# Spectral filter and 32-head attention on one core: GpSimd freed of its recurring work, and filler matmuls moved to another PSUM bank

## The chip, the cores and the metric

The kernel runs on one core of one Trainium2 chip. The metric is device time in microseconds from the first to the last instruction of the core; the figure for the kernel before is the median of three executions, and a profile of one further execution is used for the reading.

## The reference

Two independent computations of one input length, S = 2048 rows of D = 640, are joined along the last axis.

```python
def _A_ref(x, w_r, w_i):                      # part A: spectral filter
    X = rfft2(x.astype(float32), axes=(-2, -1))
    X = X * (w_r + 1j * w_i)
    return irfft2(X, s=(S, D), axes=(-2, -1)).astype(bfloat16)

def _B_ref(x, wqkv, wo):                      # part B: attention, H = 32, Dh = 20
    q, k, v = split of (x @ wqkv) by 3, heads, Dh
    p = softmax(q k^T * Dh ** -0.5)
    return (p v, heads joined) @ wo

return concatenate([A, B], axis=-1)           # 1 x 2048 x 1280, bf16
```

## The kernel before, in words

Part B is the bulk. A unit is a pair of a chunk of 512 queries and a group of 4 heads: 4 chunks by 8 groups give 32 units, each of 64 score tiles (16 key tiles by 4 heads) of 128 keys by 512 queries. A score tile is a row-tiled matmul (32 of the array's 128 rows, one head, L1724). It is turned into an exponential in one of two ways. ScalarE takes groups of 3 and 2 tiles at once from banks 0 to 2 and 3 to 5 of PSUM (L1741). VectorE takes tiles in pairs from bank 7 or 5: an eviction for each (L1814) and seven steps for the pair (L1851 to L1864) that build the exponential's bits. The exponentials meet the values in column-tiled matmuls of 32 columns a head (L1906), four heads side by side, which add up in bank 6 for the whole unit. Column 20 of each head's values is a one, so the sum of the exponentials comes out in the same bank.

A unit ends with a chain. `unit_copy` copies bank 6 to SBUF (L1925). Four small DMAs spread the sums over partitions. `unit_recip` takes their reciprocals and two extremes on VectorE (L1943 to L1946). One DMA writes them to DRAM and another spreads them over 32 partitions a head. `unit_norm` multiplies (L1964, on GpSimd in the kernel before) into `OTn`, which the output projection reads (L1986).

Part A is the 2-D transform as matmuls in stages S1 to S11. S2 loads the filter weights `Wn`, GpSimd re-lays them into `Wl` (L1104), and TensorE transposes them into `Wp` (L1121). S1 and S3 to S5 transform the input along both axes, with `Bl` transposed into `BT` by the same helper `flip_jobs`. S6 and S7 finish the forward transform and multiply by the filter (L1262, L1267, L1274). S8 to S11 go back, with `U` transposed into `UT` by `flip_jobs`. All of them are background jobs, as are the projections of Q, K and V.

The order on each engine is fixed when the program is built. The class `FK` plays the kernel on a planner's clock: `occupy` books an engine for a planned duration, `at` sets due times, and `dispatch` picks what an engine does next. For TensorE the choice is, in order, scores, a lone VectorE tile, more of a running background job (`more_bg`, up to `RUN` pieces), values, the tail, a new background job, and last `warm`, a filler matmul. `warm` and the start of background jobs of part A look at `share`, the planned use of the array over the last stretch, and act where it is at or below `WARM_SHARE`. Each engine then executes its list strictly in that order and waits on semaphores. So an instruction that waits holds up everything behind it on its engine, whatever the planner thought.

The change and the prediction also speak of `setup_B` (loads, memsets L1496 to L1515, and the padding of Q and K weights from 20 to 32 columns a head, L1511 on ScalarE for group 0 and L1513 on GpSimd for the rest), `mk_jobs_B_static` (the K projection, L1546), `job_QA` (L1623), `dummy2` (the filler, L1610) and `copy_on` (every eviction by VectorE, L227).

A second program, the class `KB`, follows for inputs whose sums leave a checked range; a flag at the end skips it here, and it takes no part in the profile.

## Time and profile before

| What | Value |
|---|---|
| time, three runs | 1002.08 us median, 969.36 to 1003.15 |
| span of the profiled run | 1016.1 us, mean granted clock of TensorE 0.844 |
| PE busy | 886.0 us (87%), 5981 matmuls |
| VectorE (DVE) busy | 838.2 us (82%), 1633 instructions |
| ScalarE (ACT) busy | 848.8 us (84%), 743 instructions |
| GpSimd (POOL) busy | 73.2 us (7%), 56 instructions |
| score tiles | 1806 on ScalarE in 723 groups, 242 on VectorE in 121 pairs |
| idle time of ScalarE before L1741 | 139.9 us, of it 81.7 for scores and 56.5 for values |
| wait of the reciprocal L1943 for its DMA | 25.9 us, 27 times |
| filler matmuls L1610 | 99 weight loads |

Busy shares are means over stretches that differ much, so they don't tell what limits a stretch; the slices and the stretches do. A group's row gives the line, the engine, the operation, shapes and count, then busy time and mean duration, then the idle time of the engine just before it and what ended that. In a timeline the bracket after an instruction is the idle time before it and what released it. PEclk is the granted clock of TensorE[...].

### The profile page before, as it was taken

The page shows a single profiled execution, that of the slowest core. Times are in us where ns is not written, and L with a number is a line of the kernel's source. Part 1 is how long each engine was busy: PE and PEld are TensorE (multiplying, and loading weights), DVE is VectorE, ACT ScalarE, POOL GpSimd, SP SyncE. Part 2 cuts the span into 40 slices and gives each one's busy share as a digit, 9 for nine tenths or more (in the row PEclk, how much of TensorE's full clock was granted, in tenths as well). Part 3 has the DMA queues.
Part 4 walks back from the last instruction along what each step waited for, and adds up shares of the span by engine and source line. Part 5 has one row for each costly group of instructions (what it writes and reads, how often), then busy time and mean ns, then how long its engine had stood idle before and what let it go on. Part 6 is the DMA issues. An engine that isn't in the chain of part 4 may idle for free.

```text
span 1016.1 us, 14983 instructions
## 1 busy us (share of the span) xinstructions
PE 886.0 (87%) x5981; PEld 279.4 (27%) x6045; DVE 838.2 (82%) x1633; ACT 848.8 (84%) x743; POOL 73.2 (7%) x56
## 2 busy tenths in 40 slices
PE   8898989779998898887999888788989999997897
PEld 4332322113233232222332111232222332222112
DVE  5677999997779898999977888888887997679983
ACT  6599988777989998999985887699887998679882
POOL 5100010220000000000000000000010010000000
PEclk9699999886779999999995877799776997579757
DMA  6240000002200000110000000101010011100000
GB/s 202 60 92 12 12 2 11 12 15 84 65 19 31 12 13 12 43 43 12 12 24 15 12 12 0 53 12 53 12 40 18 31 38 38 37 26 12 12 12 28
DMA packets 31824, 31.75 MB, mean 31 GB/s; under 512 B 13444, under 2 KB 26500, under 8 KB 31492
## 3 DMA queue, kind: packets, MB, share of 16 engines
q1 hardware_dynamic: 31748, 30.73, 10.3%
q8 instruction: 48, 0.79, 0.3%
q14 instruction: 28, 0.23, 0.1%
HBM read 24.97 MB, written 5.50 MB: 30 GB/s over the span
## 4 chain that ended last, share of the span: by engine, by line
PE 37%; DVE 36%; ACT 15%; DMA 4%; SPq 4%; issue 3%; ACTq 0%; DVEq 0%
ACT arena L1741 14%; PE ps L1724 12%; PE ps L1906 8%; DVE arena L227 6%; DVE arena L1814 6%; DMA arena<-arena 4%; SPq L361 4%; DVE arena L1855 4%; DVE arena L1859 3%; PE ps L1340 3%; DVE arena L1862 3%; DVE arena L1864 3%; DVE arena L1851 2%; DVE arena L1857 2%; DVE arena L1853 2%
## 5 line engine op out<-in xcount | busy, mean ns | idle before, releaser
L1741 ACT ACTIVATE arena<-ps 128x1536 bf16<-128x1536 f32 x723 | 837.6, 1257 | 139.9 <-PE ps L1724 81.7
L1724 PE MATMUL ps<-arena 32*128 32x512 bf16 x2048 | 344.0, 434 | 66.3 <-ACT arena L1741 41.6
L1906 PE MATMUL ps<-arena 128*32 128x512 bf16 (+1 forms) x2048 | 231.1, 444 | 15.4 <-DVE arena L1864 13.1
L1814 DVE TENSOR_SCALAR arena<-ps 128x512 uint16<-128x512 f32 x242 | 165.5, 684 | 56.5 <-PE ps L1724 55.7
L227 DVE CAST arena<-ps 128x320 bf16<-128x320 f32 (+4 forms) x262 | 146.3, 559 | 39.1 <-PE ps L1340 11.6
L1724 PEld LDWEIGHTS ps<-arena 32*128 32x128 bf16 x2048 | 74.9, 93 | 282.3 <-ACT arena L1741 175.7
L1964 POOL TENSOR_TENSOR arena<-arena 128x512 bf16<-128x512 f32 x31 | 46.4, 1496 | 881.2 <-DMA arena<-rscr 789.4
L1906 PEld LDWEIGHTS ps<-arena 128*32 128x32 bf16 (+1 forms) x2048 | 52.5, 94 | 168.1 <-issue 123.4
L1855 DVE TENSOR_TENSOR arena<-arena 128x1024 f16<-128x1024 f16 x121 | 87.7, 725 | 1.7
L1862 DVE TENSOR_TENSOR arena<-arena 128x1024 uint16<-128x1024 uint16 x121 | 87.5, 723 | 0.7
L1859 DVE TENSOR_TENSOR arena<-arena 128x1024 f16<-128x1024 f16 x121 | 84.1, 695 | 1.6
L1864 DVE TENSOR_SCALAR arena<-arena 128x1024 uint16<-128x1024 uint16 x121 | 60.2, 498 | 0.4
L1851 DVE TENSOR_SCALAR arena<-arena 128x1024 uint16<-128x1024 uint16 x121 | 55.3, 457 | 0.5
L1853 DVE TENSOR_SCALAR arena<-arena 128x1024 f16<-128x1024 int16 x121 | 53.3, 441 | 1.2
L1857 DVE TENSOR_SCALAR arena<-arena 128x1024 f16<-128x1024 f16 x121 | 53.0, 438 | 1.1
L1340 PE MATMUL ps<-arena 128*128 128x320 bf16 (+1 forms) x192 | 52.4, 389 | 0.7 <-DVE arena L227 0.3
L1623 PE MATMUL ps<-arena 128*128 128x512 bf16 x135 | 47.4, 434 | 2.1 <-issue 1.3
L1546 PE MATMUL ps<-arena 128*128 128x512 bf16 x144 | 45.2, 410 | 2.8 <-DVE arena L227 0.8
L227 DVE COPY arena<-ps 128x1024 bf16<-128x1024 bf16 (+2 forms) x54 | 33.3, 620 | 17.3 <-PE ps L539 8.0
L1986 PE MATMUL ps<-arena 128*128 128x320 bf16 x192 | 40.2, 322 | 1.6 <-DVE arena L1814 1.5
L1610 PE MATMUL ps<-arena 128*128 128x512 bf16 x85 | 36.2, 462 | 5.2 <-DVE arena L1814 4.3
L1179 PE MATMUL ps<-arena 128*128 128x328 bf16 x160 | 35.4, 320 | 5.1 <-DVE arena L1814 3.9
(74 smaller groups left out, 469.6 us busy)
## 6 DMA issues: line engine op xcount, KB each, us to landing
arena<-rscr SPq DMA_DIRECT2D x31, 256.0 KB
arena<-in_B_x_dram SPq DMA_DIRECT2D x4, 640.0 KB, 6.5
arena<-in_A_x_dram SPq DMA_DIRECT2D x4, 640.0 KB, 4.5
out_dram<-arena SPq DMA_DIRECT2D x16, 160.0 KB, 1.8
out_dram<-arena SPq DMA_DIRECT2D x4, 640.0 KB, 3.6
arena<-in_B_wqkv_dram SPq DMA_DIRECT2D x3, 700.0 KB, 9.6
arena<-f_ciCS SPq DMA_DIRECT2D x2, 1024.0 KB, 5.3
arena<-arena SPq DMA_DIRECT2D x124, 2.0 KB, 1.7
```

Of the source, the lines that this page charges most:

```text
L227: return eng.tensor_copy(out, in_)
L1340: return lambda e: e.matmul(o, l, r_, start=s_, stop=e_)
L1724: inst = e.matmul(ps[:, bank, :], kt_[32 * j:32 * j + 32, g, kt * 128:(kt + 1) * 128], q[32 * j:32 * j + 32, :], start=True, stop=True, ti ...
L1741: self.P.add("act", lambda e: e.activation(pt, in_, AF.Exp, scale=SCALE), r=[("ps", h + k) for k in range(n)], w=[("PT", i % 4)], name="exp")
L1814: self.P.add("dve", lambda e: e.tensor_scalar(v, in_, 1024.0 * SCALE * LOG2E, 32.0 * 1024 + 512, ALU.mult, ALU.add), r=[("ps", bank)], **( ...
L1851: t = self.x_op(n, one, lambda e: e.tensor_single_scalar(sh, v, 6, ALU.logical_shift_left), [kv], [ka], "x_s")
L1853: t = self.x_op(n, one, lambda e: e.tensor_scalar(t16, g, X_K / 65536.0, X_K * X_BETA, ALU.mult, ALU.add), [ka], [ka], "x_t")
L1855: t = self.x_op(n, two, lambda e: e.tensor_tensor(h16, t16, t16, ALU.mult), [ka], [kb], "x_q")
L1859: t = self.x_op(n, two, lambda e: e.tensor_tensor(h16, h16, t16, ALU.mult), [ka, kb], [kb], "x_h")
L1862: t = self.x_op(n, two, lambda e: e.tensor_tensor(v, v, h16, ALU.add), [kb, kv], [kv], "x_w")
L1864: t = self.x_op(n, one, lambda e: e.tensor_scalar(v, v, 0.125, X_BIAS, ALU.mult, ALU.add), [kv], [kv], "x_p")
L1906: inst = e.matmul(ps[32 * j:32 * j + m, 6, :], va[:, kt, 21 * h:21 * h + m], pt, start=st, stop=sp, tile_position=(0, 32 * j))
```

## The change

Its aim is that GpSimd has nothing to do while VectorE works, that VectorE and TensorE stand less behind DMAs and behind each other, and that fillers take no bank from other work.

- The filter weights are transposed straight from the layout in which they are loaded. `Wl` and its re-layout go; so does the regrouped write of `Bl`. `flip_jobs` reads its 128 columns with a stride of 41 elements, and the write into `UT` reads PSUM in another order.
- K weights are no longer padded. Each K matmul of 128 columns becomes four of 32 columns on column tiles. They read 12 columns of the next head along with each head; the zeros in the padded Q weights cancel those.
- The Q weights of groups 1 to 7 are padded on VectorE at planned times, and the memset of the output weights moves to VectorE.
- The normalize moves to VectorE. The planned times from copy to reciprocal and from reciprocal to normalize grow.
- The filler multiplies zero weights with K and adds to bank 6, where the values are summed. `share` looks back over 1.7 us instead of 2.2.
- Four settings change: LEAD 20 to 16, WARM_SHARE 0.42 to 0.44, RUN 3 to 2, PVQ 12 to 10. K jobs may be continued in the mode of the value matmuls.

```diff
@@ mk_jobs_A
-        J_s2r = {}
-        for c in range(2):
-            def s2_relayout(J, p, c=c):
...
-                P.add("pool", lambda e: e.tensor_copy(o, i_), r=[("Wn", c), ("Wnpad",), zr("A", 1)],
-                      w=[("Wl", c)] + zw("B", 1), name="wl_relayout")
...
+        self.dma(self.kron.rearrange("p m k -> p (m k)"), self.c_kron.ap(), w=[("kron",)], name="ld_kron")
@@ flip_jobs
-                            in_ = src[:, c, lb, :]
+                            in_ = src[:, c, lb, :] if src.shape[2] == 41 else src[:, c].rearrange("p k (e b) -> p b (k e)", b=41)[:, lb, :]
...
-                            in_ = in_.rearrange("p (b s e) -> p b s e", b=n, s=16)
+                            in_ = in_.rearrange("p (b s e) -> p s e b", b=n, s=16)
...
-        s2 = flip_jobs("Wp", self.Wl, lambda c, b0, n: self.Wp[:, c, b0:b0 + n, :],
-                       lambda c, b: [("Wl", c)], lambda c, b: ("Wp", c, b), zr("B", 1), zw("C", 1), {0: [J_s2r[0]], 1: [J_s2r[1]]})
+        s2 = flip_jobs("Wp", self.Wn, lambda c, b0, n: self.Wp[:, c, b0:b0 + n, :],
+                       lambda c, b: [("Wn", c), ("Wnpad",)], lambda c, b: ("Wp", c, b), zr("A", 1), zw("C", 1), [J_s2l])
...
-                    o = self.Bl[:, co].rearrange("p b (s e) -> p b s e", e=8)[:, :, sbv, :]
-                    in_ = ps[:, bank, 0:328].rearrange("p (b e) -> p b e", e=8)
+                    o = self.Bl[:, co, sbv, :]
+                    in_ = ps[:, bank, 0:328]
...
-            return self.UT[:, :, c, b0 * 8:(b0 + n) * 8].rearrange("p s (b e) -> p b s e", e=8)
+            return self.UT[:, :, c, :].rearrange("p s (e b) -> p s e b", b=41)[:, :, :, b0:b0 + n]
@@ setup_B
-        P.add("pool", lambda e: e.memset(wk5, 0.0), r=[("z", "C", 0)], w=[("wkz",)], name="ms_wk")
...
+        P.add("dve", lambda e: e.memset(zt, 0.0), w=[("zt",)], name="ms_zt")
+        P.add("dve", lambda e: e.memset(wo, 0.0), w=[("woz",)], name="ms_wo")
...
-        for g in range(NG):
-            for which, dst, key in ((1, wk, "wk"), (0, wq, "wq")):
...
-                    P.add("pool", (lambda d4, src: lambda e: e.tensor_copy(d4, src))(d4, src), r=[skey] + zk, w=[(key, g)], name="wpad")
-        P.add("pool", lambda e: e.memset(wo, 0.0), w=[("woz",)], name="ms_wo")
+        self.wpad("act", 0)
+    def wpad(self, en, g):
...
+        self.P.add(en, lambda e: copy_on(e, en, d4, src), r=[("wqkv", "q" if g else "q0"), ("z", "B", 0)], w=[("wq", g)], name="wpad")
@@ mk_jobs_B_static
-                        l = self.wk_pad[:, cbv, g, :]
...
-                        return lambda e: e.matmul(o, l, r_, start=st, stop=sp)
+                            for j in range(4):
+                                c = 640 + g * 80 + 20 * j
+                                inst = e.matmul(ps[32 * j:32 * j + 32, bank, :], self.wqkv[:, cbv, c:c + 32], r_, start=st, stop=sp, tile_position=(0, 32 * j))
...
+                J.mode = "c"
@@ dummy2
-        self.P.add("pe", lambda e: e.matmul(ps[:, bank, 0:512], k[:, 0, 0:128], k[:, 0, 0:512], start=True, stop=True),
-                   r=[("KT", 0, 0)], w=[("ps", bank)], name="dummy")
+        ps, k, z = self.ps, self.KT, self.zt.to_broadcast([128, 128])
+        self.P.add("pe", lambda e: e.matmul(ps[:, 6, :], z, k[:, 0, 0:512], start=False, stop=False, skip_group_check=True),
+                   r=[("KT", 0, 0), ("zt",)], pw=[("ps", 6)], name="dummy")
@@ unit_copy, unit_recip, unit_norm
-            self.dve_urgent.append((self.now + DMA_NS + 300.0, lambda: self.unit_recip(u)))
+            self.dve_urgent.append((self.now + 5200.0, lambda: self.unit_recip(u)))
...
-            self.pool_q.append((self.now + DMA_NS + 200.0, lambda: self.unit_norm(u), lambda: self.op_left[:u // NG].count(0) == u // NG))
+            self.dve_urgent.append((self.now + 3600.0, lambda: self.unit_norm(u), lambda: self.op_left[:u // NG].count(0) == u // NG))
...
-        self.P.add("pool", lambda e: e.tensor_tensor(o, osb, rb, ALU.mult), r=[("osb",), ("rb",)], w=[("OT", g)], name="normalize")
-        t = self.occupy("pool", 1600.0)
+        self.P.add("dve", lambda e: e.tensor_tensor(o, osb, rb, ALU.mult), r=[("osb",), ("rb",)], w=[("OT", g)], name="normalize")
+        t = self.occupy("dve", 595.0, 95.0)
@@ more_bg
-        if self.mode != "f" or self.f_run >= self.cfg["RUN"] or not self.att or self.u_pv >= 32:
+        if self.mode == "r" or self.f_run >= self.cfg["RUN"] or not self.att or self.u_pv >= 32:
...
-            if J.nxt < len(J.pe):
+            if J.nxt < len(J.pe) and J.mode == self.mode:
@@ share, warm
-        while h and h[0][0] < self.now - 2200.0:
+        while h and h[0][0] < self.now - 1700.0:
...
-        return sum(d for _, d in h) / 5280.0
+        return sum(d for _, d in h) / 4080.0
...
-        bank = self.bg_bank()
-        if bank is None:
+        if self.ps6_free > self.now or self.bank_own.get(6) is not None or not self.pv_any:
             return False
-        self.dummy2(bank)
-        self.bank_t[bank] = self.occupy("pe", self.pe_dur(216.0, "f"))
+        self.dummy2()
+        self.occupy("pe", self.pe_dur(216.0, "f"))
@@ run
+        for g in range(1, NG):
+            t = 19000.0 + 2000.0 * g
+            self.dve_urgent.append((t, lambda g=g: self.wpad_late(g)))
+            self.at(t)
@@ kernel
-    fast = FK(nc, arena, *args, cfg=dict(LEAD=20, T_A=680000.0, WARM_SHARE=0.42, RUN=3, PVQ=12))
+    fast = FK(nc, arena, *args, cfg=dict(LEAD=16, T_A=680000.0, WARM_SHARE=0.44, RUN=2, PVQ=10))
```

## The prediction

> **What bounds the kernel now.** I read three views, in this order: the busy slices with the granted clock, the same by stretches of 25 us, and the timeline just ahead of each fall of the clock.

> In the page's slices ScalarE, VectorE and TensorE all look nearly full, and GpSimd nearly empty. The row to look at is the clock: it falls again and again, and where it falls ScalarE's digits fall too.

> ```profile
> DVE  5677999997779898999977888888887997679983
> ACT  6599988777989998999985887699887998679882
> POOL 5100010220000000000000000000010010000000
> PEclk9699999886779999999995877799776997579757
> ```

> The stretches show the price. The columns are the stretch, its length, then busy time and instructions of PE, PEld, DVE, ACT and POOL, and the granted clock.

> ```profile
> 400.00:425.00 25.00, 21.35 (x168) 6.38 (x170) 23.92 (x51) 25.00 (x24) 1.27 (x1) 1.00 0.09 25
> 450.00:475.00 25.00, 20.32 (x155) 5.95 (x155) 24.01 (x53) 24.19 (x23) 1.27 (x1) 1.00 0.15 44
> 850.00:875.00 25.00, 25.00 (x118) 6.21 (x115) 15.94 (x32) 17.21 (x14) 1.34 (x1) 0.50 0.02 9
> 875.00:900.00 25.00, 24.53 (x108) 5.58 (x108) 15.30 (x32) 15.98 (x13) 1.26 (x1) 0.50 0.11 38
> ```

> At full clock ScalarE (24 or 23 exponentials) and VectorE are full together. At half clock TensorE is full, and 14 or 13 exponentials go through. I counted over the trace from 60 to 998 us: 645 us at full clock take 1331 score tiles on ScalarE and 179 on VectorE, 2.34 tiles a us; 293 us at half clock take 407 and 55, 1.58 a us. So a microsecond at half clock loses 1 - 1.58/2.34 = 0.326 us, and the 293 us cost 95 us. With none of them, this profile of 1016 us would have been 921.

> What starts a fall is in the timeline: TensorE stands for 0.6 to 5 us, because VectorE, whose order is fixed, stands. Three kinds, one of each:

> ```profile
> 188.16 4.55 POOL L1104 COPY arena<-arena 128x5248 bf16<-128x5248 bf16 x1
> 188.35 4.91 DVE L1855 TENSOR_TENSOR arena<-arena 128x1024 f16<-128x1024 f16 x1
> 194.00 0.62 PE L1724 MATMUL ps<-arena 32*128 32x512 bf16 x4 [3.22 <-DVE arena L227]
> ...
> 529.51 0.25 DVE L1943 RECIPROCAL arena<-arena 128x16 f32<-128x16 f32 x1 [1.74 <-DMA arena<-arena]
> 531.19 0.62 PE L1906 MATMUL ps<-arena 128*32 128x512 bf16 x4 [1.64 <-DVE arena L1864]
> ...
> 954.00 0.39 PE L1610 MATMUL ps<-arena 128*128 128x512 bf16 x1 [0.80 <-DVE arena L1814]
> ```

> A VectorE step that takes 0.68 us elsewhere takes 4.91 beside the GpSimd copy, and the clock is halved from 193.2. The reciprocal waits 1.74 us for the denominators' DMA; halved from 531.1 to 565.2. A filler matmul (L1610) waits for VectorE to have read its bank; halved from 954.4 to 1002.

> [...] L1855 takes 674 to 697 ns apart from GpSimd work and up to 4905 beside it.
> [...] the clock is half or full [...] only 1.00 and 0.50 occur, in lengths that are multiples of 3.41 us. [...] Weighting each matmul by its share of the array, most windows before a fall have under 0.37 here, and half-clock stretches run at about 0.33[...].
> [...]

> **The change, part by part.**

> *GpSimd.* It gives up L1104 (two copies, 9.6 us), L1513 (14 weight pads, 8.6), L1515 (a 4.36 us memset) and L1964 (31 normalizes, 46.4). Over the trace, VectorE instructions that overlap GpSimd work take 31 us longer than their like alone: 17.0 for the normalizes, 8.5 for the copies, 4.2 for the memset, 1.5 for the rest. That is removed from VectorE.

> *VectorE gains* 31 normalizes. The nearest row is L1267 (two f32 inputs in SBUF, bf16 out, 512 wide), 682 ns alone: 31 x 0.68 = 21 us. The seven pads are nearest ScalarE's 0.52 us each for the same shape: 4 us. The memset of 5120 values: L1492 wrote 656 in 0.605 us, so 4.7 us, at the start, where VectorE otherwise waits 6.85 us for the first transposes; hidden. Twelve evictions of the turned result read PSUM with a stride: between 0.68 us as now and twice that, 0 to 8 us; I take 5. Sum about 30 added against 31 removed.

> *The recip wait.* The scheduler's due time for the reciprocal goes from 2.5 to 5.2 us after the copy. The trace has it ready 3.6 us after the copy in most units, 4.3 to 5.4 in six. So the 25.9 us that L1943 waits go almost wholly.

> *The new wait.* The normalize now stands in VectorE's queue, due 5.8 us after the reciprocal's group. GpSimd started it 6.0 to 6.5 us after in 21 of 31 units, and 6.8 to 9.9 in ten (some of these for readers of OTn, not for the DMA). Behind it wait the exponential's steps and evictions, and TensorE for these. VectorE runs behind its plan anyway (L1814 683 ns against 598 planned, L1851 418 against 336), so a planned 5.8 us is some 6.5 real ones: 0 us for most units, 1 to 3 for about six; 8 us in all, bounds 0 and 25.

> *K weights.* 160 matmuls of 128 columns become 640 of 32 on four column tiles. Four value matmuls (L1906) start 3 ns apart and pass in one time of 216 to 320 ns, as the unpadded ones will; against 216 now that is 0 to 10 ns each, about 1 us, and where they adjoin L1906 they save the ~100 ns of a change of tiling (L1724 to L1906 ends 320 apart against 216 for L1623 to itself). Zero net. The pads that K0 waited for at the start go: 0.5 us.

> *Strided transposes.* 164 of 246 on L1121 read 128 values 82 bytes apart; 56 ns now. From 56 to 112: 0 to 9 us of TensorE, spread, beside exponentials; I take 3, nearly all hidden at full clock.

> *Fillers.* 99 now (weight loads of L1610). They took bank 5 or 7, from which VectorE's tiles and all background work also draw, and stood 20 us waiting for their readers. New ones add zero weights to bank 6 and take neither; they can only wait for the copy of that bank, once a unit. The threshold is 0.44 over 1.7 us instead of 0.42 over 2.2, so they and the background work come more evenly. Full array, full 512 columns: by the weighting above each counts as before, but no run of before shows a matmul with zero weights.

> **The sum.** Of the 293 us at half clock, I put to the three kinds by what stands ahead of each fall: copies 13.65 + 23.9 = 38, reciprocals 3.4 + 10.2 + 3.4 + 3.4 + 34.1 = 55, fillers 10.2 + 30.7 + 47.8 = 89. The other 111 (the chain of L1274 around 570 to 650, and 848 to 903) stay. The copies' go; of the other two I let half come back, since the new wait and the thin last stretch start falls too. Left: 111 + 27 + 44 = 182, that is 111 x 0.326 = 36 us saved. The first memset halted L1864 for 4.58 us at 25.26 and the clock for 17 us from 29.4: 4 + 17 x 0.326 = 9 us. VectorE, full with ScalarE at full clock, is rid of 26 us of waits less 8 of new ones: of these 18 us some 12 show. Together 57. The median of before is 1002, and 1002 - 57 = **945 us**.

> **Rivals.** *The clock stays up*: fillers that need no bank close nearly all low windows. From 921: less 9 for the start, less 12 for VectorE, plus 10 for what still falls: 910. For it: falls are started by single stands. Against: 111 us have other causes.
> *The normalize's wait takes the reciprocal's place*: 31 stands of 1 us or so, each able to start a fall. Then only the copies (38 x 0.326 = 12) and the start (9) are won, and UT's evictions cost 5: 986. For it: ten late units. Against: VectorE runs late itself.
> *Slower*: fillers of zeros don't hold the clock, or more of them fill TensorE. With 45% of the 938 us at half clock in place of 31%, 1972 tiles at 0.55 x 2.34 + 0.45 x 1.58 = 2.00 a us take 986 us, plus the 78 outside: 1064. For it: nothing shows that zeros count. Against: the warm-up matmuls before the start hold equal values, and the clock is 1.00 from 5.5 us on.

> **Numbers.** Forecast 0.55, clock up 0.15, normalize's wait 0.17, slower 0.13. The range 900 to 1000 leaves out the slow case and the edges of the others. Faster by over 2%: forecast and clock up, less 0.02: 0.68; within 2%: 0.19; slower 0.13.

> **What would show it.** Right: no VectorE step over 1 us beside GpSimd; L1943 with no wait; fewer than 200 us at half clock; ScalarE at 23 to 24 exponentials per 25 us. Wrong: a wait on the normalize of 20 us or more; falls with no stand before them, or half clock in stretches full of fillers, which would mean that zeros don't count; waits of TensorE on the bank-6 copy.

## The result

The changed kernel takes 923.11 us (median of four runs, 919.21 to 929.11), the kernel before 990.34 us over its four (969.36 to 1003.15). The ratio is 0.948, with a 95% interval of 0.936 to 0.960: faster. The forecast was 945 us, 900 to 1000.

The ratio leaves out executions over 1.5% longer than the fastest of their kernel, here two of the kernel before, and the profile of before is of such an execution too (1016 us); the medians give 0.932, and differences between the two profiles are larger than the 67 us between the medians.

The slices of the page after, for the rows that were shown of before:

```profile
DVE  5777999998988999999999989998887999899994
ACT  6979999999899999998999899987887999999994
POOL 1000000000000000000000000000000000000000
PEclk9989999999999999999999899985785999999999
```

GpSimd is empty after the first slice. The clock of TensorE now falls in a few places alone, and after the first slices ScalarE's row is at 8 or 9 wherever it doesn't.

The stretches of the kernel after (the columns are as before: length, then PE, PEld, DVE, ACT and POOL busy with their counts, then the granted clock):

```profile
400.00:425.00 25.00, 21.50 (x157) 6.71 (x162) 24.16 (x53) 25.00 (x24) 0.00 (x0) 1.00 0.04 12
450.00:475.00 25.00, 23.93 (x205) 10.26 (x208) 24.04 (x50) 24.05 (x22) 0.00 (x0) 1.00 0.05 16
625.00:650.00 25.00, 24.59 (x135) 7.34 (x135) 19.80 (x35) 17.25 (x16) 0.00 (x0) 0.50 0.04 12
875.00:900.00 25.00, 20.07 (x152) 5.42 (x153) 22.54 (x47) 24.94 (x23) 0.00 (x0) 1.00 0.04 12
```

The stretch 875 to 900 had 13 exponentials at half clock before and has 23 at full clock now. Where the clock still is at half (625 to 650) the old picture returns: TensorE full, 16 exponentials.

The rows of the groups that answer to those of the prediction:

```profile
L1732 ACT ACTIVATE arena<-ps 128x1536 bf16<-128x1536 f32 x725 | 829.4, 1287 | 57.5 <-PE ps L1897 34.4 <-PE ps L1715 21.7
L1601 PEld LDWEIGHTS ps<-arena 128*128 128x128 bf16 x210 | 17.1, 98 | 32.5 <-issue 30.0 <-DVE arena L1921 1.3
L1960 DVE TENSOR_TENSOR arena<-arena 128x512 bf16<-128x512 f32 x31 | 21.3, 688 | 13.7 <-DMA arena<-rscr 13.6
L1939 DVE RECIPROCAL arena<-arena 128x16 f32<-128x16 f32 x31 | 7.5, 243 | 0.3 <-DMA arena<-arena 0.3
```

ScalarE's idle time before its exponentials went from 139.9 to 57.5 us. There are 210 fillers in place of 99. The reciprocal no longer waits (0.3 us, 25.9 before), but the normalize, now on VectorE, waits 13.6 us for its DMA.

Where the time went can be counted from the two traces, over the same part as in the prediction (from 60 us to 18 us before the end). Before: 645 us at full clock and 293 at half clock for 1972 score tiles. After: 762.5 us at full clock at 2.392 tiles a us, and 78.5 at half clock at 1.618, for 1951 tiles. The 97 us between the profiles are therefore

- 70 us for the clock: 293 x 0.326 = 95.5 before, less 78.5 x (1 - 1.577/2.340) = 25.6 that are left;
- 17 us for a better rate at full clock: 1824 tiles take 762.5 us in place of 779.5 at 2.340;
- 9 us for the start: 21 tiles more are done by 60 us, 21/2.34;
- 1 us for the better rate at half clock, 1.618 against 1.577.

The price of 0.326 us is borne out by other executions. The record has the mean granted clock of each; as only 1.00 and 0.50 occur in the traces, the time at half clock is 2 x (1 - clock) x span. Over the 32 executions of the kernel before that ran beside the experiments, a straight line through time against time at half clock rises by 0.331 us for each microsecond.

### The profile page after: what moved, and what is told of

It reads as the page before. It is cut to its first block, busy times and chain, and to the rows that moved or that the text cites. A ratio compares the mean times of both kernels' runs of the same rounds, so it can differ in the third digit from the quotient of the medians.

```text
span 919.0 us, 16086 instructions
## 1 busy us (share of the span) xinstructions
PE 824.0 (90%) x6559; PEld 279.9 (30%) x6636; DVE 818.1 (89%) x1646; ACT 839.9 (91%) x744; POOL 2.9 (0%) x7
## 4 chain that ended last, share of the span: by engine, by line
ACT 53%; PE 22%; DVE 17%; DMA 6%; issue 1%; ACTq 0%; DVEq 0%
ACT arena L1732 53%; PE ps L1715 7%; PE ps L1897 5%; DVE arena L227 4%; DMA arena<-rscr 4%; DVE arena L1805 2%; DVE arena L1253 2%; DMA rscr<-arena 2%; PE ps L1305 1%; DVE arena L1258 1%; PE ps L1533 1%; PE ps L1112 1%; DVE arena L1853 1%; PE ps L1614 1%; DVE arena L1850 1%
## 5 line engine op out<-in xcount | busy, mean ns | idle before, releaser
L1732 ACT ACTIVATE arena<-ps 128x1536 bf16<-128x1536 f32 x725 | 829.4, 1287 | 57.5 <-PE ps L1897 34.4
L1715 PE MATMUL ps<-arena 32*128 32x512 bf16 x2048 | 318.5, 397 | 60.1 <-ACT arena L1732 42.9
L1897 PE MATMUL ps<-arena 128*32 128x512 bf16 (+1 forms) x2048 | 208.6, 403 | 6.6 <-DVE arena L1921 2.6
L1805 DVE TENSOR_SCALAR arena<-ps 128x512 uint16<-128x512 f32 x236 | 161.5, 685 | 29.8 <-PE ps L1715 28.3
L227 DVE CAST arena<-ps 128x512 bf16<-128x512 f32 (+4 forms) x261 | 145.4, 559 | 20.2 <-PE ps L1576 5.1
L1850 DVE TENSOR_TENSOR arena<-arena 128x1024 f16<-128x1024 f16 x118 | 80.8, 685 | 1.5
L1846 DVE TENSOR_TENSOR arena<-arena 128x1024 f16<-128x1024 f16 x118 | 80.7, 685 | 1.4
L1601 PE MATMUL ps<-arena 128*128 128x512 bf16 x156 | 55.9, 397 | 2.9 <-issue 1.9
L1842 DVE TENSOR_SCALAR arena<-arena 128x1024 uint16<-128x1024 uint16 x118 | 49.3, 419 | 0.7
L1855 DVE TENSOR_SCALAR arena<-arena 128x1024 uint16<-128x1024 uint16 x118 | 49.2, 417 | 0.4
L1533 PE MATMUL ps<-arena 128*32 128x512 bf16 x640 | 48.4, 382 | 0.6 <-ACT arena L226 0.3
L1614 PE MATMUL ps<-arena 128*128 128x512 bf16 x142 | 46.6, 399 | 1.8 <-DVE arena L1805 0.8
L227 DVE COPY arena<-ps 128x1024 bf16<-128x1024 bf16 (+2 forms) x55 | 40.2, 732 | 8.3 <-PE ps L540 4.6
L1331 PE MATMUL ps<-arena 128*128 128x320 bf16 (+1 forms) x192 | 39.8, 303 | 1.8 <-DVE arena L227 1.3
L1960 DVE TENSOR_TENSOR arena<-arena 128x512 bf16<-128x512 f32 x31 | 21.3, 688 | 13.7 <-DMA arena<-rscr 13.6
```

Of the source, the lines that this page charges most:

```text
L227: return eng.tensor_copy(out, in_)
L1533: inst = e.matmul(ps[32 * j:32 * j + 32, bank, :], self.wqkv[:, cbv, c:c + 32], r_, start=st, stop=sp, tile_position=(0, 32 * j))
L1601: self.P.add("pe", lambda e: e.matmul(ps[:, 6, :], z, k[:, 0, 0:512], start=False, stop=False, skip_group_check=True), r=[("KT", 0, 0), (" ...
L1614: return lambda e: e.matmul(o, l, r_, start=st, stop=sp)
L1715: inst = e.matmul(ps[:, bank, :], kt_[32 * j:32 * j + 32, g, kt * 128:(kt + 1) * 128], q[32 * j:32 * j + 32, :], start=True, stop=True, ti ...
L1732: self.P.add("act", lambda e: e.activation(pt, in_, AF.Exp, scale=SCALE), r=[("ps", h + k) for k in range(n)], w=[("PT", i % 4)], name="exp")
```

## Experiments

Two questions were open: which parts of the change bring this, and by which way. The prediction had it that falls of the clock are started by single stands of VectorE and so of TensorE (theory A). The rival (B) has the supply of array work hold the clock, and stands matter for themselves alone. Medians below are of four runs where nothing else is said. There were four groups of runs, on three chips. The kernel before ran beside each, with medians of 979.8 to 983.0 us in the first three and 989.3 in the last; the changed kernel, run again as a control beside one group, had 923.55 us (920.48 to 932.07, ratio 0.944).

> The changed kernel as it is, on the chip of this group of runs, as their measure. Both theories: 923 us within 5, 60 to 100 us at half clock.

### No fillers

```diff
     def warm(self):
-        if not self.att or self.all_exp():
+        if self.att or self.all_exp():
             return False
```

The condition can't be met once attention runs, so no filler is placed; nothing of the result is left out.

> The changed kernel with no filler matmuls in the attention at all. Theory A (fillers with zero weights keep the clock up): half clock rises to 150 us or more, 955 us (940 to 990). Rival Z (matmuls with zero weights don't count, what helped was only that banks 5 and 7 and the waits were freed): half clock unchanged within 40 us, 915 to 928 us.

977.5 us (963.7 to 988.0), against 923.55 for the control. The clock's row of its page:

```profile
PEclk9999999975999999859997786757755799885557
```

320 us at half clock in the part counted above, against 75 for the control. By their granted clocks all four executions were at half clock for 298 to 341 us of the whole span, those of the control for 73 to 108. So matmuls with zero weights do hold the clock, and with all the other parts in place, normalize, due times, K weights and no work on GpSimd, the clock still falls at least as much as before (195 to 284 us in the executions beside it). Rival Z is out, for no filler takes bank 5 or 7 here, and so is the idea that taking away the stands keeps the clock up by itself.

### The old filler in the changed kernel

```diff
-    def dummy2(self):
...
-        self.P.add("pe", lambda e: e.matmul(ps[:, 6, :], z, k[:, 0, 0:512], start=False, stop=False, skip_group_check=True),
+    def dummy2(self, bank):
...
+        self.P.add("pe", lambda e: e.matmul(ps[:, bank, 0:512], k[:, 0, 0:128], k[:, 0, 0:512], start=True, stop=True),
...
-        if self.ps6_free > self.now or self.bank_own.get(6) is not None or not self.pv_any:
+        bank = self.bg_bank()
+        if bank is None:
             return False
```

> The changed kernel with the filler of before: real K weights, a start of its own, in bank 7 or 5, placed only where such a bank is free. Theory A (falls of the clock are started when VectorE and then TensorE stand; fillers that wait for a VectorE read are one of three such kinds): about half of the 89 us at half clock put to the fillers come back, so 120 to 150 us at half clock, 938 us (925 to 955), with the fillers waiting 10 us or more for VectorE. Rival B (the clock is held by the supply of fillers and by the settings of the share, the stands matter little): most of the 210 us of half clock that the change removed come back, 975 us or more.

963.4 us (961.0 to 965.1), 40 us more than the control, with 147 us at half clock against 75. Its fillers and its longest waits of ScalarE, from the groups and from the waits (total, times, longest):

```profile
L1601 PEld LDWEIGHTS ps<-arena 128*128 128x128 bf16 x159 | 11.7, 98 | 33.9 <-issue 18.6 <-DVE arena L1805 10.1 <-DVE arena L227 1.2
```

```profile
ACT arena L1732 <- PE ps L1897: 56.9, 32, 18.7
```

159 fillers are placed in place of 210, and they wait 10.1 us for VectorE's reads of their bank. The clock term is what theory A said: 72 us more at half clock, 23 us at 0.326. But the time lies above its range, and under that of rival B. The rest is about as long as something that neither theory named: one stand of ScalarE of 18.7 us. It is taken up below, with the late normalize.

### The new filler alone

The kernel before with the new `dummy2` and the new condition in `warm`, and nothing else; share and settings as before.

> The kernel before with the new filler alone: zero weights added into bank 6, placed without a bank of its own; share and settings as before. If the fillers' place is what keeps the clock up (theory A as the first group of runs left it), half clock falls by 60 us or more and the time by some 22 us against the kernel before, ratio 0.97 to 0.985. Rival: without the other parts the stands of VectorE go on starting falls and nothing is won, ratio 0.99 to 1.01.

940.2 us (937.1 to 944.5), ratio 0.959 (0.952 to 0.966): 40 us won by this one part. The clock's row, the fillers and the reciprocal:

```profile
PEclk9899998979999999897799989999999999999989
```

```profile
L1613 PEld LDWEIGHTS ps<-arena 128*128 128x128 bf16 x178 | 14.6, 99 | 28.9 <-issue 26.0 <-DVE arena L1929 1.5
L1947 DVE RECIPROCAL arena<-arena 128x16 f32<-128x16 f32 x31 | 7.8, 253 | 24.6 <-DMA arena<-arena 24.6
```

That is more than the 22 us that theory A expected of it. The stands are all there: the reciprocal waits 24.6 us, and beside the two GpSimd copies two steps of VectorE take 4.44 and 4.67 us, behind which TensorE stands for 7.8 us. Yet only 85 us in the part counted are at half clock. Falls still start, 12 against 18 in the profile of before, but they last 7 us in the mean in place of 16. At an unchanged threshold 178 fillers are placed where there were 99; none has to find a free bank. So it is the supply of array work that holds the clock, as rival B said, and a stand alone isn't enough for a long fall. By the granted clocks, the median at half clock is 205 us in the kernel before beside it and 93 here; at 0.326 that is 37 of the 40 us. The freed banks 5 and 7 alone don't do it, since they are as free in the run without fillers. Whether what counts is the number of fillers or that they come without waiting was not separated.

### The reciprocal due early again

```diff
-            self.dve_urgent.append((self.now + 5200.0, lambda: self.unit_recip(u)))
+            self.dve_urgent.append((self.now + 2500.0, lambda: self.unit_recip(u)))
...
```

> The changed kernel with the reciprocal due 2.5 us after the copy instead of 5.2, as before. Theory A: the reciprocal again waits some 25 us for its DMA, falls of the clock start behind these waits, 130 to 150 us at half clock; with the lost VectorE time 945 us (935 to 960). Rival B: the wait shows only itself where VectorE is full, 5 to 10 us, and half clock stays under 100 us: 930 us.

947.0 us (943.9 to 949.4): 24 us more than the changed kernel. The time is theory A's, the way is not:

```profile
L1939 DVE RECIPROCAL arena<-arena 128x16 f32<-128x16 f32 x31 | 7.8, 253 | 28.2 <-DMA arena<-arena 28.1
```

The wait is back with 28.1 us, but half clock is 72 us in the part counted, as in the changed kernel (78.5). What fell is the rate at full clock, from 2.392 to 2.331 tiles a us; on 1851 tiles that is 20 us. Six tiles fewer by 60 us are some 3 more. So in this plan the waits cost most of what they last, 20 of 28 us, and don't touch the clock while the fillers hold it. That VectorE has no slack at full clock would explain it, but this is not shown: the order of the plan changed with the edit, and the run with the normalize on GpSimd, below, has as low a rate (2.333) with no wait of VectorE for these DMAs.

### Filler and due time together, GpSimd as before

The kernel before with the new filler and the reciprocal due at 5.2 us; the re-layout, the pads, the memset and the normalize stay on GpSimd.

> The kernel before with two parts of the change alone: the new filler, and the reciprocal due 5.2 us after the copy. GpSimd keeps all its work. Theory D (these two are the change; taking work from GpSimd adds little): the 40 us of the filler alone and the 24 us of the due time add, 918 us (910 to 928), ratio 0.94. Theory A (GpSimd's locks are a third part, some 20 us): 935 us (930 to 942), ratio 0.955.

929.95 us, but spread from 918.5 to 933.5, between the ranges of the two theories; ratio 0.943 (0.929 to 0.958), where the control has 0.944. The two parts win 53 us against the kernel before that ran beside them (982.96), where the control won 56 against its own (979.82). By the medians, 929.95 and 923.55, some 6 us are left for all the rest of the change, and the intervals don't exclude that the rest is worth nothing.

Against the run with the new filler alone, the reciprocal's wait is gone:

```profile
L1947 DVE RECIPROCAL arena<-arena 128x16 f32<-128x16 f32 x31 | 7.5, 242 | 0.0
```

Here that is worth 10 us by the medians, 13 by the gains over the kernels before beside them, and not 24, and the rate at full clock stays (2.354 tiles a us, 2.352 with the filler alone). So what a wait of VectorE costs depends on the plan around it.

### GpSimd's work put back into the changed kernel

First the normalize alone, on GpSimd as before:

```diff
-        self.P.add("dve", lambda e: e.tensor_tensor(o, osb, rb, ALU.mult), r=[("osb",), ("rb",)], w=[("OT", g)], name="normalize")
+        self.P.add("pool", lambda e: e.tensor_tensor(o, osb, rb, ALU.mult), r=[("osb",), ("rb",)], w=[("OT", g)], name="normalize")
...
```

The rest of the edit gives GpSimd its queue in the plan again. The due time stays at 3.6 us; in the kernel before it was 2.4.

> The changed kernel with the normalize back on GpSimd, all else as changed. Theory A: VectorE loses 21 us of normalizes and 13.6 us of waits on their DMA, and gets about 17 us of lock by GpSimd, so it has some 18 us less to do: no difference, 915 to 930 us, half clock as in the changed kernel within 40 us. Rival C [...]: single VectorE steps of 1 us and more start falls, 945 us or more.

934.95 us (931.8 to 938.3), 11 us more than the control, with less half clock (48 us). Its steps of the exponential and the waits of ScalarE:

```profile
L1846 DVE TENSOR_TENSOR arena<-arena 128x1024 f16<-128x1024 f16 x122 | 86.7, 711 | 1.7
L1853 DVE TENSOR_TENSOR arena<-arena 128x1024 uint16<-128x1024 uint16 x122 | 86.3, 707 | 0.8
```

```profile
ACT arena L1732 <- PE ps L1897: 52.9, 33, 16.9
```

In the changed kernel:

```profile
L1846 DVE TENSOR_TENSOR arena<-arena 128x1024 f16<-128x1024 f16 x118 | 80.7, 685 | 1.4
```

The steps are 711 and 707 ns in the mean in place of 685, with the normalizes of GpSimd beside them; over all of VectorE that is 19 us, close to the 17 us counted in the trace of before. No fall comes of it. One stand of ScalarE of 16.9 us is in this run too, and is more than the difference in time. So the run doesn't show that moving the normalize pays, nor that it costs.

Then two copies of the filter weights onto themselves on GpSimd, in the place of the re-layout:

```diff
+            def s2_again(J, p, c=c):
+                o = self.Wn[:, c].rearrange("p k l -> p (k l)")
+                self.P.add("pool", lambda e: e.tensor_copy(o, o), r=[("Wnpad",), zr("A", 1)], w=[("Wn", c)], name="w_again")
...
```

> The changed kernel with two GpSimd copies of the filter weights onto themselves, 5248 values a partition each, where the re-layout stood; the transposes wait for them as before. Theory A: each locks a VectorE step for 4 to 5 us, ScalarE and TensorE stand for 3 to 5 us each, and each starts a fall of the clock of 10 to 24 us: 943 us (932 to 955), half clock 35 us more than the control. Rival: the stands cost only themselves, 930 us, no fall within 10 us of either copy.

933.1 us (926.2 to 940.1), between the two. The timeline around both copies:

```profile
48.38 4.56 POOL L1104 COPY arena<-arena 128x5248 bf16<-128x5248 bf16 x1 [15.30 <-DMA arena<-in_A_w_r_dram]
48.88 4.34 DVE L1848 TENSOR_SCALAR arena<-arena 128x1024 uint16<-128x1024 uint16 x1
...
53.59 0.69 PE L1582 MATMUL ps<-arena 128*128 128x240 bf16 x5 [2.51 <-DVE arena L227]
...
59.60 4.56 POOL L1104 COPY arena<-arena 128x5248 bf16<-128x5248 bf16 x1 [6.67 <-DMA arena<-in_A_w_i_dram]
...
60.94 3.50 DVE L1848 TENSOR_SCALAR arena<-arena 128x1024 uint16<-128x1024 uint16 x1
...
66.01 0.58 PE L1582 MATMUL ps<-arena 128*128 128x240 bf16 x4 [2.40 <-DVE arena L227]
```

Steps of 0.42 us become 4.34 and 3.50 us, TensorE stands 2.5 and 2.4 us behind them, and the clock is at half from 56.3 and from 66.5. This is the sequence of the prediction. But these falls last 3.4 and 10.2 us, and falls come near this place without copies too: in the control from 62.8 us for 6.8, in the run with the early reciprocal from 55.4 for 3.4. Half clock is only 7 us more than the control's in the part counted. So steps held up like this bring no long fall; whether they bring a short one isn't shown. Nor need the 10 us between this run and the control be the copies': ScalarE stands for 13.3 us at one place of this run, from 604 to 617 us, far from them.

### The settings

```diff
-    fast = FK(nc, arena, *args, cfg=dict(LEAD=16, T_A=680000.0, WARM_SHARE=0.44, RUN=2, PVQ=10))
+    fast = FK(nc, arena, *args, cfg=dict(LEAD=20, T_A=680000.0, WARM_SHARE=0.42, RUN=3, PVQ=12))
...
-        return sum(d for _, d in h) / 4080.0
+        return sum(d for _, d in h) / 5280.0
```

> The changed kernel with the five old settings: LEAD 20, WARM_SHARE 0.42 looked back over 2.2 us, RUN 3, PVQ 12. Theory A: settings are second to the stands, 930 us (918 to 942), half clock 80 to 130 us. Rival B: the share of array use that the plan holds decides whether the clock falls; 150 us or more at half clock, 950 us or more.

931.7 us, spread from 923.8 to 940.8, with 58 us at half clock in the profiled execution: by the medians the settings are worth some 8 us, and within the spread perhaps nothing. In the other direction, the threshold at 0.47:

> The changed kernel with the threshold of the share at 0.47 instead of 0.44: more fillers. If the fillers' number is what still holds back the clock, half clock falls from 80 to under 40 us and the time by 10 us or more, 912 us. Rival: the falls that are left start in the chain of the filter stage (L1265), where TensorE waits for VectorE and no filler is in the plan's way; half clock stays at 60 us or more, and more fillers cost TensorE: 920 to 932 us.

932.3 us (922.9 to 934.5), 297 fillers and 65 us at half clock. More fillers than the change has bring nothing, as the rival said; ScalarE stands once for 14.2 us in this run, more than the 9 us between it and the control.

### The wait of the normalize, and what hid it

```diff
-            self.dve_urgent.append((self.now + 3600.0, lambda: self.unit_norm(u), lambda: self.op_left[:u // NG].count(0) == u // NG))
+            self.dve_urgent.append((self.now + 5400.0, lambda: self.unit_norm(u), lambda: self.op_left[:u // NG].count(0) == u // NG))
...
```

> The changed kernel with the normalize due 5.4 us after its DMA instead of 3.6, so that VectorE need not wait. If a VectorE wait costs what the reciprocal's cost (28 us of wait, 24 us of time), the 13 us of wait are worth 11 us: 912 us (906 to 918). Rival: the wait stands where VectorE has slack, or the later normalize delays the output projection: 920 to 930 us.

922.96 us (917.3 to 924.4): no gain. But the wait is gone (2.0 us), and half clock fell to 26 us in the part counted, both of which should have shown. The group of the normalize, then the timeline of the place where the time went:

```profile
L1960 DVE TENSOR_TENSOR arena<-arena 128x512 bf16<-128x512 f32 x31 | 21.2, 682 | 2.0 <-DMA arena<-rscr 2.0
```

```profile
476.50 1.42 DVE L1253 TENSOR_TENSOR arena<-ps,arena 128x512 f32<-128x512 f32 x2
...
477.84 0.68 DVE L227 CAST arena<-ps 128x512 bf16<-128x512 f32 x1
478.44 0.42 DVE L1855 TENSOR_SCALAR arena<-arena 128x1024 uint16<-128x1024 uint16 x1
...
479.37 1.41 DVE L1253 TENSOR_TENSOR arena<-ps,arena 128x512 f32<-128x512 f32 x2
...
480.69 1.41 DVE L1258 TENSOR_TENSOR arena<-arena 128x512 bf16<-128x512 f32 x2
482.02 0.68 DVE L1921 COPY arena<-ps 128x512 f32<-128x512 f32 x1
...
483.80 3.28 ACT L1732 ACTIVATE arena<-ps 128x1024 bf16<-128x1024 f32 x3 [18.40 <-PE ps L1897]
```

In the filter's multiplication (L1253, L1258) VectorE takes every eviction that is ready before the exponential's steps. The last pairs of the unit whose values are being summed come late, that unit can't end, the buffers of ScalarE's exponentials stay full of the next unit's, and ScalarE stands 18.4 us. A stand at the same stage, while L1253 runs, appears with 18.7, 16.9, 14.2 and 13.3 us in four runs above, with 11.0 in the run without fillers, and with 9.9 in the profile of before. Each edit makes the planner lay out another order, and some orders hold it.

The last experiment takes it away: VectorE goes on with the steps of the unit that is being finished, while ScalarE is a unit ahead of it.

```diff
         if e == "dve":
+            u = self.u_pv
+            if self.u_act > u and ((self.x_pair is not None and self.x_pair[0][0] == u) or any(c[3][0][0] == u for c in self.x_run)):
+                if self.dve_q(self.dve_urgent) or self.try_x_step() or self.try_x_first():
+                    return True
             return (self.dve_q(self.dve_urgent) or self.try_bg_ev("dve") or self.try_x_first() or self.try_x_step() or self.vmax())
```

> The kernel with the normalize due 5.4 us after its DMA, and one more rule for VectorE's order: while ScalarE is a unit ahead of the values, the exponential's steps of the unit that is being finished go ahead of background evictions. Theory E (in the run with the later normalize the saved wait was hidden by ScalarE standing 18.4 and 6.2 us, because VectorE served the filter stage first and the unit's last values were missing): no stand of ScalarE over 6 us before the tail, and 903 us (896 to 911). Rival: the stands are slack that returns elsewhere, 917 to 925 us.

915.9 us (median of six, 911.7 to 924.7), where the kernel before had 989.3 us beside it (969 to 1005 over eleven); ratio 0.944 (0.934 to 0.954), by the medians 0.926. The waits of ScalarE:

```profile
ACT arena L1732 <- PE ps L1897: 25.7, 22, 3.8
ACT arena L1732 <- PE ps L1715: 24.1, 30, 2.3
```

The long stand is gone, the longest left is 3.8 us, and ScalarE's idle time before its exponentials is 50.8 us in place of 62.8. This fits theory E; but several plans without the rule have no such stand either, the control's among them. The time is 7 us under that of the run before it, not the 20 expected, and nearer to the rival. By the medians this is the fastest of all the kernels, but it ran on another chip than the control, and its ratio to the kernel before is the control's; so it isn't shown to beat the changed kernel.

## Why the prediction was right, and which steps of it were not

**What bounds the kernel** held: at full clock ScalarE and VectorE together (25.00 and 24.16 of 25 us busy in the stretch from 400), at half clock TensorE (24.59 of 25 from 625), and the half clock as the largest single loss. Its price of 0.326 us for each microsecond accounts for 70 of the 97 us between the profiles.

**The sum** came out, but in part by luck. In the control's group the kernel before takes 979.8 us, with 205 us at half clock, and the changed kernel 923.6, with 80: 56 us, of which 125 x 0.326 = 41 are the clock's. The forecast was a gain of 57, of which 36 + 17 x 0.326 = 42 for the clock. But it took 111 + 17 us at half clock from an execution that had 318 in all and left the rest, where a usual one has 205 and 80 are left: two errors of about 100 us at half clock cancel. The 22 us between 945 and 923 are those between the median of three, 1002, from which the forecast counted, and 980.

**What the falls were put down to** is the step that failed. The prediction put each fall, with its whole length, down to the stand just ahead of it, and shared out 293 us: 38 to GpSimd's copies, 55 to the reciprocals, 89 to fillers, the rest fixed. Stands do lie ahead of most falls: in the trace of before, 14 of 18 follow a window of 3.41 us in which TensorE stands for 0.6 us or more. But 26 other such windows are followed by none. In the kernel with the new filler alone nearly all stands remain and the long falls don't, and in the kernel with no fillers the stands of reciprocal and GpSimd are gone and there are 16 falls of 20 us in the mean. So the fillers, for which 45 of 89 us at half clock were counted as won, some 15 us of time, are worth 40 us alone and 54 against none. That is the mis-sized term. What stands and fillers have in common is the work that the array gets in a window: in the traces 55 of the 58 emptiest windows at full clock are followed by half clock, and none of the 2742 fullest (the last section has the counts).

**The reciprocal's wait** was put at 12 us for VectorE's time together with the rest, and some 9 us for the clock (28 us at 0.326). Put back into the changed kernel it cost 24 us, none of them by the clock; taken out of the kernel with the new filler it won 10 to 13. The split was wrong, and the size stays open between these.

**The new wait** of the normalize was put at 8 us with bounds of 0 and 25, and is 13.6. That its removal brought nothing by itself isn't settled: with it came a stand of the planner's making.

**GpSimd**: 31 us removed and 30 added for VectorE was right in kind. VectorE is busy 818 us after and 838 before, with six tiles fewer. The filler and the due time without it reach 930 us, so all that the words "GpSimd without steady work" stand for is some 6 us, no more than the spread of these runs, where the falls put down to its copies alone were counted with 38 x 0.326 = 12.

**The small terms.** The memset on VectorE took 2.19 us, not 4.7, and is hidden; seven pads 0.28 us each, not 0.52. Ten full evictions into `UT` take 1.23 us in place of 0.69, 5 us in all, as taken. At full clock strided transposes follow each other every 62 ns in place of 56, 1 us for all 164, where 3 were taken (of a bound at twice the 56, the author's guess); their weight loads are longer (138 in place of 109 ns in the mean over all transposes) and hidden. 640 K matmuls are busy 48.4 us, against 45.2 recorded for 144 of the 160 before. The 9 us for the start came as worked out.

**The rivals.** "The clock stays up" was nearest in its mechanism, fillers that need no bank close most of the low windows (4 at full clock under 0.36 of the time filled, 20 before), and in its number too: 910 lies nearer to 923 than 945 does. Of "the normalize's wait takes the reciprocal's place" the wait came, with 13.6 us, but not the falls. "Slower, since zeros don't count" is refuted by the run without fillers (320 us at half clock, against 75).

## What to carry to other kernels

An event that lies just ahead of each loss needn't be what the size of the loss depends on: count also where the same event does no harm, and take away the other candidate. What a wait in front of a full engine costs is a matter of the plan around it: 28 us of waits put back cost 24, 24.6 taken away won 10 to 13, and 11.6 of the normalize's taken away won nothing by themselves, so try it both ways. Count a forecast from an execution like those it will be compared with; here the profile had 318 us at half clock and a usual execution 205. In a kernel whose order is planned, an edit changes the order everywhere; look for single long stands of the bounding engine before a few microseconds are put down to the edit.

## What the runs showed of the hardware

In the traces of before and after only 1.00 and 0.50 occur as granted clock. Each stretch at half clock lasts a multiple of 3.41 us (3.41 to 54.61 before, 6.83 to 37.55 after), but for the last, which the end cuts off. At half clock a matmul of 512 columns (L1623 of before) follows another of its line after 400 ns in place of 216, and one of 80 columns (L1564) after 67 in place of 36 (medians).

All fourteen traces were therefore cut into windows of 3.41 us. Each matmul was weighted by its share of the array, as in the prediction (those that a trace lacks put in from their weight loads), from 60 us to 18 us before the end. Of 58 windows at full clock in which the matmuls so weighted fill under 0.30 of the time, 55 are followed by a window at half clock; of 294 between 0.30 and 0.42, 52; of 2742 with more, none, though TensorE stands for 0.6 us or more in 118 of these. So in these traces a stand goes with a fall where the window's work is low, and with the new fillers fewer windows are in that range: of those at full clock 20 lie under 0.36 in the trace of before, 17 without fillers, and 4 in the changed kernel.

Zeros added into the bank in which the values are summed cost next to no wait for a bank: the weight loads of all 210 wait for VectorE for 1.3 us together (L1601 above), where the fillers of the run with the old form waited 10.1 for L1805. An eviction of 128x1024 bf16 from PSUM that reads with a stride, and writes in another order, took 1.23 us against 0.69 us in order, and a memset of 128x5120 bf16 zeros on VectorE ran as 2560 words of 32 bits in 2.19 us where GpSimd had taken 4.36.
